# Halves' differences read from PSUM by VectorE, weight low parts issued one by one, and other slots for roundings and maxima

## The chip, the cores and the metric

The kernel runs on one core of one Trainium2 chip. The metric is the device time of one execution in microseconds (us), smaller is better. Engine names are those of the profile: PE is TensorE (PEld its weight loads), DVE is VectorE, ACT is ScalarE, POOL is GpSimd, SP is SyncE, which here issues DMAs alone.

## The reference

A gated linear attention feeds a mixture of experts that is evaluated densely: every token goes through every expert, and a Sinkhorn-balanced matrix `P` weights the outputs.

```python
# attention: batch 4, heads 8, sequence 768, head size 48; f = sigmoid(f_logit)
for t in range(S):
    state = f[:, :, t, :, None] * state + einsum('bhd,bhe->bhde', k[:, :, t], v[:, :, t])
    y[:, :, t] = einsum('bhd,bhde->bhe', q[:, :, t], state)
# experts: x is y as 3072 tokens x 384, 8 experts of 1024 hidden units
logits = x @ w_gate
P = exp(logits - logits.max())
for _ in range(8):
    P /= P.sum(1, keepdims=True) + 1e-9
    P /= P.sum(0, keepdims=True) + 1e-9
    P *= N / E
for e in range(E):
    out += P[:, e:e + 1] * (maximum(x @ w1[e], 0) @ w2[e])
```

## The kernel before

All matrix products run on PE in fp16 with each operand split in a high part (the fp16 rounding, made by ACT) and a low part (what the rounding left, made by DVE or POOL); a product is three matmuls: high x high, high x low, low x high. The names end in h and l for the two parts.

The kernel has three stages. In the first, until about 490 us, the attention runs beside experts 0 and 1, whose outputs go to DRAM and are added later ("readds"). The second and longest is a loop of 48 **periods**, `ORDER`: experts 2 to 7, each in two halves `m` of its hidden units, each half over the four batches `b`. The third is a short tail that finishes the last period's blocks.

A period computes 256 x 768-token work in two layers.

- **Layer one** is a 3x3 block scheme with 15 products in place of 27. `SLOTS` gives their order and the PSUM bank (`kb_A` to `kb_F`) that each is added to: a period has 15 **slots**, one product of 6 matmuls of 256 columns each (two 128-row chunks `c`, three part pairs). Products are used in several sums, so between the slots banks are copied, added and rounded. `EVENTS` says after which slot's matmuls which of these is issued; numbers of 15 and more fall in the next period. Kinds: `copy` (ACT, `cp`), `add`, `init`, `sum` (DVE, from PSUM and a copy), `move` (ACT), `hs` (ACT: relu of a bank to `kr`, fp32), `hh`/`hl` (ACT/DVE: relu's high part `kh` and low part `kl`).
- **Layer two** takes three blocks of tokens `t` (0, 1, 2) per period, each by seven products in place of eight (a 2x2 scheme with halves of 192 columns). It needs sums and differences of halves of the relu: `gs` 1 to 3 (DVE, from the bank and `kr`, to `kr` and `kf`), `gd` (the difference of the two halves of `kr`, on POOL for t = 0 and 1, on DVE for t = 2), `ga`, `gf`, `gb` (`kah` and `kal`, one quarter's parts), and `gh`/`gl` (ACT/POOL: high parts `kgh` and low parts `kgl` of `kr` and `kf`). `paired` is a generator with the products of one block; `advance` steps it twice per slot, the block starting 21, 26 and 31 slots after the period's begin for t = 0, 1, 2. Its results are scaled and added by DVE (`yy`, `acc`), ACT (`xx`, `part`, copies inside `kyps` and `kxps`) and POOL (`acc`).

**Weights** for a later period are prepared meanwhile, on the slots that the plan lists (a list counts from an even period's slot 0 and runs on through the next). `prepare_w1` issues per step: the load (SP); four groups of subtractions (POOL, `k1s`); the maximum (DVE, `wmx`); three steps of high parts (ACT, `k1h`); the low parts `k1l` (DVE): first half of the ten sums, second half, and then both groups of single blocks in one step. `prepare_w2`: load; maximum; two high parts (ACT, `k2h`); two steps of subtractions (POOL, `k2s`); both low parts of single blocks in one step (DVE, `k2l`); high part of the sums; low part of the sums. Periods 0, 1 and 3 have lists of their own, since the loop starts without a store of weights. On the plan stand too the readds (`again`: DMA, ACT `yz`, POOL `acc`), the checks of the inputs' ranges (`checks`) and maxima of the weights of experts 0 and 1 (`maxima`: load in one step, DVE maximum in the next).

What sets the order: every instruction is pinned behind the one issued before it on its engine (`pin`, `mm`), so each engine runs exactly the order in which the code of `period` issues: a slot's matmuls, its events, the first step of the block, the previous period's events that are due (`pending`), the second step of the block, the plan's jobs. Only semaphores hold an engine back. Banks A and F share one PSUM buffer in a period, three such buffers rotate among A, F, E and C; B and D have one each. `kr` has three buffers, `kf` two, raw weights three (`wraw`, shared by loads and `k2s`).

Of the kernel before, what the change touches and what calls it, by code (L numbers as in the profile page):

```python
# [12 lines left out]
ALU = mybir.AluOpType  # L13
# [4 lines left out]
B, H, S, D = 4, 8, 768, 48  # L18
NP = H // 2
C = 64  # L20
# [17 lines left out]
W1S = 2.0 ** 6  # L38
# [26 lines left out]
         (7, 'C', 0), (10, 'D', 0), (8, 'B', 0), (5, 'C', 0), (3, 'D', 0), (14, 'F', 0))  # L65
LAST = (12, 8, 5, 3, 11, 14)
EVENTS = {1: (('copy', 'A', 4),), 2: (('copy', 'B', 13),), 3: (('add', 'A', '-', 13),), 4: (('copy', 'A', 6), ('copy', 'B', 1)),
# [7 lines left out]
END = 24  # L75
ORDER = [(e, m, b) for e in range(2, NE) for m in range(2) for b in range(B)]
PAIRED = (0, 1, 2)
BY_POOL = (1,)
# [180 lines left out]
def fast(ctx, tc, qkf, vbd, wg, w1, w2, out, flag):  # L259
    nc = tc.nc  # L260
# [17 lines left out]
    def pin(ins):  # L278
        engine = ins.ins.engine
        if fixed[0]:  # L280
            if engine in last:
                behind(ins, last[engine])
            last[engine] = ins
        return ins
# [24 lines left out]
    for h in range(2):  # L309
        nc.gpsimd.affine_select(  # L310
            out=mask[h * 64:(h + 1) * 64], in_=mask[h * 64:(h + 1) * 64],
# [701 lines left out]
    def prepare_w1(e, j, cuts=(3, 5, 8)):  # L1013
        raw = raw_weights(e, 1, j)
        yield
        sums = kw.tile([128, 10, 128], F32, name=f"k1s_{e}_{j}", tag="sums", bufs=1)

        def block(v):
            if isinstance(v, str):
                q = int(v[1])  # L1020
                return raw[:, q // 2, 128 * (q % 2):128 * (q % 2) + 128]
            return sums[:, WPOS.index(v), :]

        for part in (WSUMS[i:k] for i, k in zip((0,) + cuts, cuts + (None,))):
            for r, p, op, q in part:
                pin(nc.gpsimd.tensor_tensor(out=block(r), in0=block(p), in1=block(q), op=ALU.add if op == '+' else ALU.subtract))  # L1026
            yield
        pin(nc.vector.tensor_reduce(out=wmx[:, 0, 4 * e + j:4 * e + j + 1], in_=raw.rearrange("p a f -> p (a f)"), axis=AX.X, op=ALU.max, apply_absolute_value=True))
        yield
        wh, wl = (kw.tile([128, PRODUCTS, 128], F16, name=f"k1{n}_{e}_{j}", tag=f"k1{n}") for n in "hl")  # L1030
        halves = ((slice(0, 5), sums[:, 0:5]), (slice(5, 10), sums[:, 5:10]))
        ones = ((slice(10, 12), raw[:, 0:2, 0:128]), (slice(12, 15), raw[:, 0:3, 128:256]))
        for parts in (halves[:1], halves[1:], ones):
            for at_, src in parts:
                pin(nc.scalar.activation(out=wh[:, at_, :], in_=src, func=AF.Copy, scale=W1S))
            yield
        for parts in (halves[:1], halves[1:], ones):
            for at_, src in parts:
                pin(nc.vector.scalar_tensor_tensor(out=wl[:, at_, :], in0=src, scalar=W1S, in1=wh[:, at_, :], op0=ALU.mult, op1=ALU.subtract))  # L1039
            if parts is ones:  # L1040
                k1[e, j] = wh, wl
            yield

    def prepare_w2(e, j):
# [4 lines left out]
        wh, wl = (lp.tile([128, 7, DH], F16, name=f"k2{n}_{e}_{j}", tag=f"k2{n}", bufs=4) for n in "hl")  # L1049
        (b11, b12), (b21, b22) = ((raw[:, f, 0:DH], raw[:, f, DH:DM]) for f in range(2))  # L1050
        pieces = ((wh[:, 0, :], wl[:, 0, :], b11), (wh[:, 1:3, :], wl[:, 1:3, :], raw[:, 1, :].rearrange("p (r d) -> p r d", d=DH)))
# [10 lines left out]
        def lows(parts):  # L1062
            for h_, l_, src in parts:
                pin(nc.vector.scalar_tensor_tensor(out=l_, in0=src, scalar=W2S, in1=h_, op0=ALU.mult, op1=ALU.subtract))  # L1064

        lows(pieces)
        yield
        pin(nc.scalar.activation(out=wh[:, 3:7, :], in_=sums, func=AF.Copy, scale=W2S))
        yield
        lows(((wh[:, 3:7, :], wl[:, 3:7, :], sums),))  # L1070
# [173 lines left out]
    def at_slots(n, slots, gen):  # L1244
        for s in slots:
            plan.setdefault((n, s), []).append(lambda: next(gen, None))

    again = readds()
# [4 lines left out]
    def at_all(n, slots, gen):  # L1253
        for slot in slots:
            at_slots(n + slot // PRODUCTS, (slot % PRODUCTS,), gen)

    for n, (e, m, b) in enumerate(ORDER):
        part = n % 4
        if n + 4 < PERIODS and part in (0, 2):
            e2, m2, _ = ORDER[n + 4]  # L1260
            gen = prepare_w1(e2, 2 * m2 + part // 2)
            at_all(n, (0, 3, 4, 5, 6, 8, 9, 10, 11, 22, 23, 24) if n else (14, 17, 18, 19, 20, 24, 25, 26, 27, 28, 29, 37), gen)
        if n == 0:
            at_all(0, (1, 2, 4, 5, 6, 8, 9, 12), prepare_w2(e, 2 * m))
            at_all(0, (4, 6, 8, 10, 13, 14, 14, 16), prepare_w2(e, 2 * m + 1))
        if n - part + 4 < PERIODS and (n in (1, 3) if n < 4 else part in (0, 2)):
            e2, m2, _ = ORDER[n - part + 4]
            at_all(n, (10, 22, 25, 26, 27, 29, 35, 38) if n != 3 else (0, 2, 8, 12, 13, 16, 17, 20), prepare_w2(e2, 2 * m2 + part // 2))
        if n >= FIRST_READD:
            at_slots(n, (9, 12), again)  # L1270
        if n >= 5 and part in (1, 3):
            for s in (0, 4):
                plan.setdefault((n, s), []).append(lambda: next(checks, None))
        if n >= 6 and part in (0, 2):
            at_slots(n, (1, 9), maxima)
        if n == PERIODS - 2:
            at_slots(n, (1, 2, 3), judged)
    at_all(1, (1, 3, 6, 8, 11, 13, 14, 18, 21, 23, 26, 28, 29), converts[3])
# [11 lines left out]
    def event(ctxt, ev):  # L1290
        banks_, copies, hs, tag = ctxt
# [32 lines left out]
        elif kind == 'gd':  # L1324
            r = hs['r', ev[1]]
            pin((nc.gpsimd if ev[2] == 'P' else nc.vector).tensor_tensor(out=r[:, 0], in0=r[:, 1], in1=r[:, 0], op=ALU.subtract))  # L1326
        elif kind == 'ga':
            hs['a', ev[2]] = [lp.tile([128, 2, 128], F16, name=f"ka{q}_{tag}_{ev[2]}", tag=f"ka{q}{ev[2]}", bufs=1) for q in "hl"]
            pin(nc.scalar.activation(out=hs['a', ev[2]][0], in_=bk[:, :, 0:128], func=AF.Relu))
# [129 lines left out]
```

## Time and profile before

| | |
|---|---|
| median of 3 runs | 1549.83 us (1549.19 to 1549.98) |
| profiled execution, its own time | 1550.04 us |
| its span (first to last instruction) | 1548.3 us |
| granted TensorE clock, mean | 0.996 |
| first write of the period loop to kb_A | 493.39 us |
| start of period 4, of period 46 | 576.40 us, 1475.33 us |

The profile is of one execution. Busy time of an engine leaves out waiting; a matmul's end is modelled, so its row is longer (0.24 to 0.27 us) than the step from one matmul to the next. A timeline row has the start, the duration, engine, line, operation, output and inputs by the program's names, shape, and in brackets the idle time before it with what ended it. A group's row has the count, the busy time, the mean in ns of one, and idle time before it. A wait's row has the total in us, how often, and the longest.

### The profile page before, as it was taken

To read this page: it belongs to the slowest core of one execution; us is meant where nothing else is said; L and a number is where in the kernel's file an instruction comes from. 1 tells how busy PE (TensorE), PEld (TensorE's weight loads), DVE (VectorE), ACT (ScalarE), POOL (GpSimd) and SP (SyncE) were. 2 spreads that over 40 slices of the span, in tenths; PEclk is the share of its full clock that TensorE was granted. 3 is DMA by queue.
4 is the path that set the end of the run, shared out by engine and by line. 5 is a ranking of instruction groups with operands and counts; after the bars stand their busy time and mean duration, and the time that the engine had idled before them with its cause. 6 is when DMAs were issued, how large, how long until landed. Compare 5 with 4: busy or idle time off the path is not lost.

```text
span 1548.3 us, 40171 instructions
## 1 busy us (share of the span) xinstructions
PE 1475.1 (95%) x16051; PEld 1264.8 (82%) x16051; DVE 1315.3 (85%) x2510; ACT 1038.4 (67%) x2310; POOL 1066.0 (69%) x1197
## 2 busy tenths in 40 slices
PE   7899999999999799999999999999999999999996
PEld 4688876676666689898888888898889888988995
DVE  8888888985775998889899999888988989888776
ACT  6655556553344677787777777787777777777772
POOL 1244434546437676989998888898988777887761
PEclk9999999999999999999999999999999999999999
DMA  9455555531000101112221121111111101000011
GB/s 279 118 127 133 126 137 120 142 94 29 31 32 32 32 22 38 44 53 58 62 63 55 40 63 43 48 41 47 47 32 33 32 22 32 22 12 12 2 58 69
DMA packets 82805, 96.00 MB, mean 62 GB/s; under 512 B 49872, under 2 KB 66384, under 8 KB 82608
## 3 DMA queue, kind: packets, MB, share of 16 engines
q1 hardware_dynamic: 82608, 93.34, 21.9%
q8 instruction: 127, 2.08, 0.6%
q14 instruction: 70, 0.57, 0.1%
HBM read 69.53 MB, written 14.16 MB: 54 GB/s over the span
## 4 chain that ended last, share of the span: by engine, by line
PE 54%; DVE 31%; POOL 5%; ACT 5%; issue 4%; DMA 0%; DVEq 0%; POOLq 0%; ACTq 0%
PE kyps L287 13%; PE yps L287 13%; PE hps L287 10%; PE kb_A L287 5%; DVE k1l L1039 4%; PE kb_B L287 4%; DVE kf L1323 3%; DVE kl L1351 2%; POOL kgl L1346 2%; DVE yy L1182 2%; DVE k2l L1064 2%; POOL k1s L1026 2%; DVE kr L1326 2%; PE kb_D L287 2%; DVE kr L1323 2%
## 5 line engine op out<-in xcount | busy, mean ns | idle before, releaser
L287 PEld LDWEIGHTS <-k1h 128*128 128x128 f16 x2880 | 282.0, 98 | 40.5 <-DVE kl L1351 11.2
L287 PE MATMUL kyps<-k2h,kgh 128*128 128x192 f16 x1152 | 283.6, 246 | 1.0 <-ACT kyps L1179 1.0
L287 PE MATMUL kyps<-k2l,kgh 128*128 128x192 f16 x1152 | 283.7, 246 | 0.0
L287 PE MATMUL kyps<-k2h,kgl 128*128 128x192 f16 x1152 | 283.7, 246 | 0.0
L287 PEld LDWEIGHTS <-kgh 128*128 128x128 f16 x2304 | 216.8, 98 | 3.2
L1346 POOL TENSOR_TENSOR kgl<-kr,kgh 128x512 f16<-128x512 f32 x141 | 166.5, 1181 | 48.5 <-ACT kgh L1343 48.4
L1346 POOL TENSOR_TENSOR kgl<-kf,kgh 128x512 f16<-128x512 f32 x141 | 180.3, 1279 | 4.7 <-ACT kgh L1343 4.7
L1182 DVE SCALAR_TENSOR_TENSOR yy<-kyps,pes,part 128x192 f32<-128x192 f32 x264 | 108.3, 410 | 85.3 <-PE kyps L287 82.7
L287 PEld LDWEIGHTS <-k1l 128*128 128x128 f16 x1440 | 141.0, 98 | 38.3 <-issue 28.5
L1218 POOL TENSOR_TENSOR acc<-acc,yy 128x384 f32<-128x384 f32 x129 | 141.4, 1096 | 42.0 <-DVE yy L1182 42.0
L287 PE MATMUL yps<-w2h,hl 128*128 128x384 f16 x384 | 125.2, 326 | 4.0 <-DVE hl L440 3.8
L287 PE MATMUL yps<-w2l,hh 128*128 128x384 f16 x384 | 125.1, 326 | 2.3 <-DVE w2l L359 2.3
L287 PEld LDWEIGHTS <-w1h 128*128 128x128 f16 x1344 | 97.3, 98 | 34.9 <-issue 4.0
L287 PE MATMUL yps<-w2h,hh 128*128 128x384 f16 x384 | 125.1, 326 | 0.2 <-ACT hh L437 0.2
L1179 ACT ACTIVATE kxps<-kyps 128x192 f32<-128x192 f32 x144 | 46.6, 324 | 105.4 <-DVE acc L1182 58.7
L287 PEld LDWEIGHTS <-kgl 128*128 128x128 f16 x1152 | 112.8, 98 | 4.6 <-issue 1.2
L287 PEld LDWEIGHTS <-hh 128*128 128x128 f16 x768 | 74.5, 98 | 48.1 <-issue 2.9
L287 PEld LDWEIGHTS <-kh 128*128 128x128 f16 x1152 | 108.3, 98 | 3.2
L1218 POOL TENSOR_TENSOR acc<-acc,xx 128x384 f32<-128x384 f32 x43 | 43.0, 1000 | 74.8 <-ACT xx L1179 74.8
L287 PE MATMUL kyps<-k2h,kh 128*128 128x192 f16 x288 | 70.7, 246 | 22.5 <-DVE yy L1182 21.0
L1343 ACT ACTIVATE kgh<-kr 128x512 f16<-128x512 f32 x144 | 90.7, 630 | 2.0 <-DVE kr L1323 1.9
L1343 ACT ACTIVATE kgh<-kf 128x512 f16<-128x512 f32 x144 | 90.5, 629 | 0.3 <-PE kyps L287 0.3
(298 smaller groups left out, 5406.9 us busy)
## 6 DMA issues: line engine op xcount, KB each, us to landing
q<-in_qkf_dram SPq DMA_DIRECT2D x23, 672.0 KB, 5.1
vr<-in_vbd_dram SPq DMA_DIRECT2D x24, 384.0 KB, 3.7
k1r<-in_w_dram SPq DMA_DIRECT2D x24, 384.0 KB, 3.0
ys<-yr SPq DMA_DIRECT2D x48, 192.0 KB, 2.8
k2r<-in_w_dram SPq DMA_DIRECT2D x24, 384.0 KB, 3.1
yb<-ys SPq DMA_DIRECT2D x48, 192.0 KB, 2.4
out_dram<-acc SPq DMA_DIRECT2D x24, 192.0 KB, 1.9
w1r<-in_w_dram SPq DMA_DIRECT2D x8, 384.0 KB, 10.7
```

The source lines that it names most:

```text
L287: ins = (nc.tensor.transpose if transpose else nc.tensor.matmul)(**kw)
L1026: pin(nc.gpsimd.tensor_tensor(out=block(r), in0=block(p), in1=block(q), op=ALU.add if op == '+' else ALU.subtract))
L1039: pin(nc.vector.scalar_tensor_tensor(out=wl[:, at_, :], in0=src, scalar=W1S, in1=wh[:, at_, :], op0=ALU.mult, op1=ALU.subtract))
L1064: pin(nc.vector.scalar_tensor_tensor(out=l_, in0=src, scalar=W2S, in1=h_, op0=ALU.mult, op1=ALU.subtract))
L1179: pin(nc.scalar.activation(out=out, in_=in_, func=AF.Copy, **kw))
L1182: pin(nc.vector.scalar_tensor_tensor(out=y, in0=ps, scalar=p, in1=z, op0=ALU.mult, op1=ALU.add))
L1218: pin((nc.vector if n == len(ORDER) - 1 else nc.gpsimd).tensor_tensor(out=y, in0=y, in1=z.rearrange("p s d -> p (s d)"), op=ALU.add))
L1323: pin(nc.vector.scalar_tensor_tensor(out=out, in0=bk[:, :, 128 * v:128 * v + 128], scalar=0.0, in1=other, op0=ALU.max, op1=op))
L1326: pin((nc.gpsimd if ev[2] == 'P' else nc.vector).tensor_tensor(out=r[:, 0], in0=r[:, 1], in1=r[:, 0], op=ALU.subtract))
L1343: pin(nc.scalar.activation(out=hs['g', t][0][i], in_=hs['f' if i else 'r', t], func=AF.Copy))
L1346: pin((nc.vector if tag == str(PERIODS - 1) else nc.gpsimd).tensor_tensor(out=hs['g', t][1][i], in0=hs['f' if i else 'r', t], in1=hs['g', ...
L1351: pin(nc.vector.scalar_tensor_tensor(out=hl, in0=bk, scalar=0.0, in1=hh, op0=ALU.max, op1=ALU.subtract))
```

## The change

- A new event kind `gp` replaces `gd` for t = 0 and t = 2: DVE computes the difference from the bank's second half and the first half of `kr` in one pass. `gd` stays for t = 1, on POOL.
- `EVENTS`: init E one slot later; ga A and hs A together at slot 8; copy of C and gf A at slot 9; hh B and init F at slot 11; hs E at slot 12; the three `gs` of B over slots 12 and 13; `gd` 1 at 14; `gl` 0 0 from slot 14 to 16; `gh` 2 0 from 22 to 21; `gl` 1 0 from 19 to 21, `gl` 1 1 from 20 to 22, `gl` 2 0 from 22 to 26; `hl` C between two `gs` at slot 18.
- `prepare_w1` issues its four low parts in four steps, `prepare_w2` its two low parts of single blocks in two.
- The plan's slots become named lists with other values; readds move from slots 9 and 12 to 9 and 14, checks from 0 and 4 to 3 and 3, maxima from 1 and 9 to 0 and 5.

```diff
-          5: (('init', 'E', '-', 6, 'D'),), 6: (('copy', 'A', 0),), 7: (('add', 'B', '+', 0),), 8: (('move', 'C', 'B'), ('hs', 'A', 0)),
-          9: (('ga', 'A', 0), ('gd', 0, 'P')), 10: (('copy', 'C', 7), ('gf', 'A', 0)), 11: (('add', 'D', '-', 7), ('hs', 'E', 1)),
-          12: (('init', 'F', '+', 1, 'D'), ('hh', 'B', 0), ('ga', 'E', 1)), 13: (('gs', 'B', 0, 1), ('gs', 'B', 0, 2), ('gs', 'B', 0, 3), ('gb', 1, 'P'), ('gd', 1, 'P')),
-          14: (('gh', 0, 0), ('gl', 0, 0), ('sum', 'D', '-', 4, 3), ('hl', 'B', 0)), 15: (('add', 'C', '+', 3), ('hh', 'D', 2), ('gh', 0, 1), ('gl', 0, 1)),
-          16: (('hs', 'F', 2), ('hh', 'C', 1), ('hl', 'D', 2)), 17: (('ga', 'F', 2), ('gd', 2, 'V'), ('gs', 'D', 2, 1), ('gs', 'D', 2, 2), ('gs', 'D', 2, 3)),
-          18: (('gs', 'C', 1, 1), ('gs', 'C', 1, 2), ('gs', 'C', 1, 3), ('hl', 'C', 1), ('gf', 'F', 2)), 19: (('gh', 1, 0), ('gl', 1, 0)),
-          20: (('gh', 1, 1), ('gl', 1, 1)), 22: (('gh', 2, 0), ('gl', 2, 0)), 23: (('gh', 2, 1), ('gl', 2, 1))}
-END = 24
+          6: (('copy', 'A', 0), ('init', 'E', '-', 6, 'D')), 7: (('add', 'B', '+', 0),), 8: (('move', 'C', 'B'), ('ga', 'A', 0), ('hs', 'A', 0)),
+          9: (('copy', 'C', 7), ('gp', 'A', 0), ('gf', 'A', 0)), 11: (('add', 'D', '-', 7), ('hh', 'B', 0), ('init', 'F', '+', 1, 'D')),
+          12: (('hs', 'E', 1), ('ga', 'E', 1), ('gs', 'B', 0, 1)), 13: (('gs', 'B', 0, 2), ('gs', 'B', 0, 3), ('gb', 1, 'P')),
+          14: (('gh', 0, 0), ('sum', 'D', '-', 4, 3), ('hl', 'B', 0), ('gd', 1, 'P')),
+          15: (('add', 'C', '+', 3), ('hh', 'D', 2), ('gh', 0, 1), ('gl', 0, 1)),
+          16: (('hs', 'F', 2), ('hh', 'C', 1), ('gl', 0, 0), ('hl', 'D', 2), ('gp', 'F', 2)),
+          17: (('ga', 'F', 2), ('gs', 'D', 2, 1), ('gs', 'D', 2, 2), ('gs', 'D', 2, 3)),
+          18: (('gs', 'C', 1, 1), ('gs', 'C', 1, 2), ('hl', 'C', 1), ('gs', 'C', 1, 3), ('gf', 'F', 2)), 19: (('gh', 1, 0),), 20: (('gh', 1, 1),),
+          21: (('gh', 2, 0), ('gl', 1, 0)), 22: (('gl', 1, 1),), 23: (('gh', 2, 1), ('gl', 2, 1)), 26: (('gl', 2, 0),)}
+END = 27
+W1AT = (1, 3, 4, 5, 5, 5, 10, 10, 11, 21, 23, 24, 25)
+W1AT0 = (16, 17, 17, 19, 20, 22, 22, 23, 25, 26, 26, 33, 37)
+W2AT = (8, 22, 23, 24, 27, 29, 30, 37, 38)
+W2AT0 = (0, 1, 5, 6, 7, 8, 9, 11, 13)
+W2AT1 = (7, 8, 8, 12, 12, 12, 14, 14, 18)
+W2AT3 = (2, 3, 11, 16, 17, 19, 19, 20, 24)
+READDAT = (9, 14)
+CHECKAT = (3, 3)
+MAXAT = (0, 5)
 ...
-        for parts in (halves[:1], halves[1:], ones):
-            for at_, src in parts:
-                pin(nc.vector.scalar_tensor_tensor(out=wl[:, at_, :], in0=src, scalar=W1S, in1=wh[:, at_, :], op0=ALU.mult, op1=ALU.subtract))
-            if parts is ones:
+        for at_, src in halves + ones:
+            pin(nc.vector.scalar_tensor_tensor(out=wl[:, at_, :], in0=src, scalar=W1S, in1=wh[:, at_, :], op0=ALU.mult, op1=ALU.subtract))
+            if src is ones[1][1]:
                 k1[e, j] = wh, wl
             yield
 ...
-        lows(pieces)
-        yield
+        for piece in pieces:
+            lows((piece,))
+            yield
 ...
-            at_all(n, (0, 3, 4, 5, 6, 8, 9, 10, 11, 22, 23, 24) if n else (14, 17, 18, 19, 20, 24, 25, 26, 27, 28, 29, 37), gen)
+            at_all(n, W1AT if n else W1AT0, gen)
-            at_all(0, (1, 2, 4, 5, 6, 8, 9, 12), prepare_w2(e, 2 * m))
-            at_all(0, (4, 6, 8, 10, 13, 14, 14, 16), prepare_w2(e, 2 * m + 1))
+            at_all(0, W2AT0, prepare_w2(e, 2 * m))
+            at_all(0, W2AT1, prepare_w2(e, 2 * m + 1))
-            at_all(n, (10, 22, 25, 26, 27, 29, 35, 38) if n != 3 else (0, 2, 8, 12, 13, 16, 17, 20), prepare_w2(e2, 2 * m2 + part // 2))
+            at_all(n, W2AT if n != 3 else W2AT3, prepare_w2(e2, 2 * m2 + part // 2))
-            at_slots(n, (9, 12), again)
+            at_slots(n, READDAT, again)
-            for s in (0, 4):
+            for s in CHECKAT:
-            at_slots(n, (1, 9), maxima)
+            at_slots(n, MAXAT, maxima)
 ...
+        elif kind == 'gp':
+            r = hs['r', ev[2]]
+            pin(nc.vector.scalar_tensor_tensor(out=r[:, 0], in0=bk[:, :, 128:256], scalar=0.0, in1=r[:, 0], op0=ALU.max, op1=ALU.subtract))
```

## The prediction

> **What bounds the kernel now.** I read the page's first part, then a table of stretches, then who waited for whom in the steady stage, then single instructions. Page, busy time by engine:
>
> ```profile
> span 1548.3 us, 40171 instructions
> PE 1475.1 (95%) x16051; PEld 1264.8 (82%) x16051; DVE 1315.3 (85%) x2510; ACT 1038.4 (67%) x2310; POOL 1066.0 (69%) x1197
> ```
>
> TensorE carries the span. The change touches only the stage of 48 periods, which begins at 493.39 us; I cut it at first writes to kb_A (columns: stretch, length, then busy time of PE, PEld, DVE, ACT, POOL):
>
> ```profile
> 493.39:576.40 83.01, 71.17 (x680) 63.13 (x679) 71.62 (x132) 57.72 (x127) 50.86 (x62) 0.96 0.09 27
> 576.40:1475.33 898.93, 869.27 (x9074) 805.05 (x9073) 796.88 (x1572) 682.57 (x1571) 760.89 (x867) 1.00 0.13 39
> 1049.91:1070.62 20.71, 20.54 (x219) 19.22 (x217) 17.98 (x37) 17.85 (x40) 19.39 (x26) 1.00 0.17 50
> 1070.62:1092.80 22.18, 20.95 (x219) 19.12 (x218) 20.23 (x40) 15.65 (x38) 19.37 (x20) 1.00 0.15 45
> 1475.33:1495.55 20.22, 20.22 (x219) 19.19 (x217) 15.13 (x41) 14.08 (x33) 12.74 (x14) 1.00 0.17 60
> 1515.77:1541.43 25.66, 17.27 (x194) 15.79 (x191) 20.60 (x53) 8.93 (x23) 4.15 (x5) 1.00 0.20 72
> ```
>
> These are periods 0 to 3; periods 4 to 45; the even period 26; the odd period 27; period 46, in which no weights are prepared; and the tail after the last kb_F product. Period 46 shows the floor: 20.22 us with PE never idle, at a granted clock of 1.00. The 42 periods of the second row take 898.93 - 42 x 20.22 = 49.7 us more than that, 2.37 per pair. An even period loses 0.49, an odd one 1.96. Periods 0 to 3 hold 83.01 - 71.17 = 11.8 us of PE idle, the tail 8.4. Nothing beyond these 70 us can be won, and no single engine but PE is full: DVE is at 89% in the steady stage. So what matters is which DVE pass comes late. Waits of PE, then of its weight loads, in the steady stage:
>
> ```profile
> PE kyps L287 <- DVE yy L1182: 15.8, 21, 1.3
> PE kb_A L287 <- ACT cp L1300: 5.0, 21, 0.3
> PE kb_D L287 <- DVE kb_F L1305: 3.8, 20, 0.2
> ```
> ```profile
> PEld L287 <- DVE kl L1351: 6.6, 19, 0.4
> ```
>
> The idle times start at modelled matmul ends, so by starts they are some 0.16 us longer each. The first row is the odd period's: DVE brings the yy of slot 10 too late for the products of slot 12. The timeline of DVE in odd period 25, and PE beside it:
>
> ```profile
> 1039.87 0.42 DVE L1182 SCALAR_TENSOR_TENSOR yy<-kyps,pes,part 128x192 f32<-128x192 f32 x1 [1.42 <-PE kyps L287]
> 1040.20 0.41 DVE L1182 SCALAR_TENSOR_TENSOR acc<-kyps,pes,acc 128x192 f32<-128x192 f32 x1
> 1040.53 0.81 DVE L1039 SCALAR_TENSOR_TENSOR k1l<-k1s,k1h 128x640 f16<-128x640 f32 x1
> 1041.26 0.95 DVE L1047 TENSOR_REDUCE wmx<-k2r 128x1 f32<-128x768 f32 x1
> 1042.12 0.81 DVE L1039 SCALAR_TENSOR_TENSOR k1l<-k1s,k1h 128x640 f16<-128x640 f32 x1
> 1042.85 2.38 DVE L1039 SCALAR_TENSOR_TENSOR k1l<-k1r,k1h 128x256 f16<-128x256 f32 x2
> 1045.16 0.41 DVE L1332 SCALAR_TENSOR_TENSOR kal<-kb_A,kah 128x256 f16<-128x256 f32 x1
> 1045.49 0.40 DVE L1182 SCALAR_TENSOR_TENSOR acc<-kxps,pes,acc 128x192 f32<-128x192 f32 x1
> 1045.82 0.40 DVE L1182 SCALAR_TENSOR_TENSOR yy<-kyps,pes,part 128x192 f32<-128x192 f32 x1
> 1046.14 0.68 DVE L1302 TENSOR_TENSOR kb_D<-kb_D,cp 128x512 f32<-128x512 f32 x1
> 1046.86 0.70 DVE L1305 TENSOR_TENSOR kb_F<-kb_D,cp 128x512 f32<-128x512 f32 x1
> ```
> ```profile
> 1045.31 0.27 PE L287 MATMUL kb_C<-xal,k1h 128*128 128x256 f16 x1
> 1046.27 0.24 PE L287 MATMUL kyps<-k2h,kh 128*128 128x192 f16 x1 [0.69 <-DVE yy L1182]
> 1047.61 0.27 PE L287 MATMUL kb_D<-xah,k1h 128*128 128x256 f16 x1 [0.19 <-DVE kb_F L1305]
> ```
>
> DVE idles 1.42 us, then runs 7.7 us without a gap, with all four k1l low parts in the middle; PE stops twice behind it, at slot 12 (yy) and at slot 13 (kb_F).
>
> **The change part by part.** *The differences.* Per period, 'gd' 0 leaves POOL and 'gd' 2 leaves DVE; each becomes a 'gp' on DVE that reads the bank. The rows for both forms, in the steady stage; gp is nearest to the kr<-kb_D pass, of the same shapes:
>
> ```profile
> L1326 DVE TENSOR_TENSOR kr<-kr 128x256 f32<-128x256 f32 x42 | 36.0, 858 | 6.7 <-ACT kr L1315 6.7
> L1323 DVE SCALAR_TENSOR_TENSOR kr<-kb_D,kr 128x256 f32<-128x256 f32 x42 | 17.8, 425 | 1.4
> L1039 DVE SCALAR_TENSOR_TENSOR k1l<-k1r,k1h 128x256 f16<-128x256 f32 x20 | 27.2, 1358 | 0.0
> L1039 DVE SCALAR_TENSOR_TENSOR k1l<-k1r,k1h 128x384 f16<-128x384 f32 x20 | 21.8, 1090 | 0.0
> ```
> ```profile
> L1326 POOL TENSOR_TENSOR kr<-kr 128x256 f32<-128x256 f32 x83 | 66.7, 804 | 3.2
> ```
>
> DVE: -0.858 + 2 x 0.425, so nothing in total; POOL: -0.80 per period. But the place matters. The old pass varies widely; in odd period 27 it was long, and stands right before the chain to kb_A of slot 5:
>
> ```profile
> 1073.86 1.40 DVE L1326 TENSOR_TENSOR kr<-kr 128x256 f32<-128x256 f32 x1 [0.35 <-ACT kr L1315]
> ```
>
> There 1.40 becomes 0.42. The gp of F keeps the wait of that row: it stands at slot 16, ACT's kr of F ends it, and the gs of D, yy and kb_A's add are queued behind it on DVE, as they were behind gd; the gp of A at slot 9 waits for ACT's kr of A, which ends a slot before. Nothing is added for either, at most the 0.35 of the row per period.
>
> The Trainium skill, page "SBUF — State Buffer", section "Who interferes with whom", says that a VectorE instruction with two SBUF inputs and a GpSimd instruction that reads SBUF block each other whole, while one with a single SBUF input goes free. The spread of kr<-kr against the steady 0.42 of the PSUM form agrees; by that rule alone gp would keep 0.42 under any POOL load, the value that the row gives as well.
>
> *k1l apart (slots 22, 23, 24 to 21, 23, 24, 25).* In the odd period the first half goes to slot 6, into the 1.42 us idle (start to start 1041.26 - 1040.53 = 0.73, cover 1.42); the last part goes behind the yy of slot 10 (about 1.0 by its row); gp of A enters at slot 9 (start to start 0.33, as kal's). yy ends 0.73 + 1.0 - 0.33 = 1.40 earlier: 1046.22 becomes 1044.82, before PE is free at 1045.31 + 0.11 = 1045.42. The wait of 0.85 at slot 12 goes. Next late is kb_F: everything still lies ahead of it, so it gains 0.73 - 0.33 = 0.40 only, to 1047.16. PE would be there at 1045.42 + 0.99 = 1046.41 (period 46, 20.22 us, is 90 matmuls of 0.11 and 126 of 0.082, so 12 products take 0.99). So slot 13 waits 0.75 where the two places together cost 1047.61 - 1046.41 = 1.20. Moving init F to slot 11 changes nothing here, as DVE had nothing between it and the add.
>
> *Odd period, the rest: 1.96 - 1.20 = 0.76* (kb_A at slot 5, kb_B at slot 1 behind kl). kb_A's chain loses 1.0 of gd; kl of B no longer stands behind POOL's kr, and one 'gs' moves from slot 13 to 12. I take both as gone.
>
> *Even period: 0.49.* The second k2l piece moves behind the add to C, so the copies of slots 2 to 4 are earlier; but it stays ahead of kb_A's add. I keep 0.35 at slot 5, and 0.1 for init E, now at slot 6 behind two maxima moved to slot 5 where DVE was idle.
>
> The k1l and k2l parts alone may each meet a POOL instruction, where two of them now stand back to back (1.36 and 1.09 above show that they already do). I put 0.1 more on the odd chain. A pair then loses 0.75 + 0.1 + 0.35 + 0.1 = 1.3 in place of 2.37: 1.07 x 21 = 22 us. Ends: nothing gained (0) and all of it (49.7).
>
> *POOL's lows.* 'gl' 1 0, 1 1, 2 0 go two to four slots later, ten k1s subtractions come first; costed at nothing, the cover is in the second rival. ACT's reordering ('ga', 'hh B', copy of C one slot earlier) fills idle time of an engine at 76% of the stage; nothing. DMA: loads of W1 at slot 1, maxima at slot 0, W2 at slot 8; SP only waits for a free buffer, and k1r's is freed by the k2l piece at slot 0, one slot before. k1s lies two slots behind it on POOL. Nothing, up to 1 us per even period if POOL waits.
>
> *Periods 0 to 3.* New slots spread W2's passes (old: a maximum at slot 2 of period 3, ahead of kb_A's add). Of 11.8 idle I take 3, between -3 and 8.
>
> *Tail.* Low parts of t=1 stood before the yy that PE waits for:
>
> ```profile
> 1526.11 0.24 PE L287 MATMUL kyps<-k2h,kh 128*128 128x192 f16 x1 [1.97 <-DVE yy L1182]
> ```
>
> They go one slot behind it; 1.97 at most, some returns; I take 1.5, from -1 to 4.
>
> Sum: 22 + 3 + 1.5 = 26.5. The profiled execution took 1550.04 us (1.7 around its span), 0.2 above the median of 1549.83, so 1523.5 in either.
>
> **The rivals.** *1. The low parts, standing alone, meet POOL each time.* For: kr<-kr at 858 on average; against: half parts at 0.81 with POOL busy. Three parts on the odd chain (second half, both others) each longer by 0.25 make 0.75, of which 0.1 is in the sum: 0.65 x 21 = 14 back, 1537. The skill's lock rule would do just this, as a pass with two SBUF inputs that starts behind POOL waits for the whole instruction.
>
> *2. Slower: kgl of t=1 too late in even periods.* Rows of POOL in period 26:
>
> ```profile
> 1059.55 1.15 POOL L1346 TENSOR_TENSOR kgl<-kr,kgh 128x512 f16<-128x512 f32 x1
> 1060.66 0.44 POOL L1026 TENSOR_TENSOR k1s<-k1s,k1r 128x128 f32<-128x128 f32 x1
> ...
> 1062.71 1.17 POOL L1026 TENSOR_TENSOR k1s<-k1s 128x128 f32<-128x128 f32 x1
> ```
> PE's slot 11 there began with this row:
> ```profile
> 1065.03 0.27 PE L287 MATMUL kb_B<-xah,k1h 128*128 128x256 f16 x1
> 1065.14 0.27 PE L287 MATMUL kb_B<-xah,k1l 128*128 128x256 f16 x1
> ```
>
> It ended at 1060.70 after three k1s. With all ten first it ends seven later: six near 0.44 and one of 1.17, some 3.8, at 1064.5. PE needs it in the second product of slot 11: 1065.03 + 6 x 0.11 + 6 x 0.082 = 1066.2, about 0.6 earlier with what PE gains until there (0.45 of odd period 25, 0.14 of 26). The margin is 1.1 us. POOL 2.9 us later (two kgl and a k1s more ahead of it) would cost 1.8 x 21 = 38 us: 1562. Against: POOL loses a kr pass (0.80) per period, and nothing new stands ahead of that kgl but the k1s.
>
> *3. The wait only moves.* If slot 13 takes all that slot 12 gave, and slot 5 stays: 1549. For: DVE runs 7.7 us without a gap; against: 0.73 of it goes into idle time.
>
> **How the numbers follow.** The sum 0.74, the first rival 0.12, no change 0.06, the slower one 0.08. A gain of 14 us less reaches 1538, of 4 us in all 1546; the other end, a pair that keeps 0.6, gains 37 + 5 and gives 1508. The range 1507 to 1544 leaves about 2 in 10 out. Differences under 0.2% (3 us) can't be told here. Faster 0.86 (the first two), same 0.06, slower 0.08.
>
> **What would show it.** Right: kyps <- yy nearly gone in the steady stage, kb_D <- kb_F larger (some 0.6 by its row per odd period); no DVE kr<-kr; the reading of the bank near 425 ns; POOL's kr<-kr 48, not 96; odd periods near 21.1 us, even near 20.7. Wrong: a row PE kyps <- POOL kgl; k1l parts of 640 elements well over 0.83 us; kb_E or kb_C waited for in even periods; periods 0 to 3 above 83 us.

## The result and the profile after

The kernel after takes 1492.34 us (median of 4 runs, 1491.92 to 1492.5) against 1549.51 (1548.87 to 1549.98): a ratio of 0.963, 95% interval 0.961 to 0.965. It is faster, as forecast, but by 57 us where 26.5 were forecast, and below the range of 1507 to 1544.

The first part of its page:

```profile
span 1490.5 us, 40081 instructions
PE 1453.7 (98%) x16051; PEld 1265.0 (85%) x16051; DVE 1283.4 (86%) x2558; ACT 1035.7 (69%) x2310; POOL 1010.9 (68%) x1149
```

PE does the same matmuls and is busy 98% of a shorter span. The stretches that answer to those of before (periods 0 to 3; 4 to 45; odd period 25; even period 26; 46; from period 47's start to the last product; columns as before):

```profile
496.25:570.72 74.47, 67.46 (x679) 61.31 (x678) 67.40 (x136) 57.75 (x127) 43.06 (x54) 1.00 0.10 31
570.72:1421.73 851.01, 850.08 (x9076) 806.53 (x9073) 770.53 (x1615) 679.54 (x1571) 717.45 (x828) 1.00 0.14 41
997.11:1017.33 20.22, 20.22 (x218) 19.20 (x217) 18.91 (x40) 15.64 (x38) 16.57 (x18) 1.00 0.14 41
1017.33:1037.55 20.22, 20.22 (x218) 19.19 (x217) 17.91 (x40) 17.56 (x41) 19.80 (x25) 1.00 0.20 60
1421.73:1441.95 20.22, 20.22 (x219) 19.20 (x217) 15.21 (x43) 14.35 (x33) 12.09 (x13) 1.00 0.17 61
1441.95:1483.75 41.80, 37.49 (x409) 34.98 (x407) 32.63 (x83) 23.27 (x56) 15.81 (x17) 1.00 0.20 73
```

Odd and even periods now take the floor of 20.22 us. The 57.8 us of span divide into: steady stage 898.93 to 851.01, -47.9 (42 periods at the floor of 20.22 are 849.2, so 1.8 are left above it); periods 0 to 3 -8.5; from period 47's start to the last product 44.63 to 41.80, -2.8; behind the last product -1.4 (not taken apart); and ahead of the loop, which begins at 496.25 in place of 493.39, +2.9. The next two rows are all that PE still waits for an engine in the steady stage, where before had rows of 15.8, 5.0 and 3.8 us and one of 6.6 for the weight loads:

```profile
PE kyps L298 <- DVE yy L1193: 0.6, 1, 0.6
PE kb_C L298 <- ACT kb_C L1319: 0.3, 1, 0.3
```

Where the odd period's 2 us went is seen on DVE and POOL side by side. First POOL beside the DVE rows of period 25 that the prediction shows, and the 128x256 low part of that stretch alone; then DVE and POOL in the same period after:

```profile
1042.16 1.79 POOL L1346 TENSOR_TENSOR kgl<-kf,kgh 128x512 f16<-128x512 f32 x1
1042.85 1.38 DVE L1039 SCALAR_TENSOR_TENSOR k1l<-k1r,k1h 128x256 f16<-128x256 f32 x1
1043.92 0.90 POOL L1326 TENSOR_TENSOR kr<-kr 128x256 f32<-128x256 f32 x1
```
```profile
1008.49 0.42 DVE L1193 SCALAR_TENSOR_TENSOR yy<-kyps,pes,part 128x192 f32<-128x192 f32 x1
...
1010.01 0.81 DVE L1049 SCALAR_TENSOR_TENSOR k1l<-k1s,k1h 128x640 f16<-128x640 f32 x1
1010.74 0.41 DVE L1340 SCALAR_TENSOR_TENSOR kr<-kb_A,kr 128x256 f32<-128x256 f32 x1
1011.08 0.41 DVE L1346 SCALAR_TENSOR_TENSOR kal<-kb_A,kah 128x256 f16<-128x256 f32 x1
1011.41 0.72 DVE L1049 SCALAR_TENSOR_TENSOR k1l<-k1r,k1h 128x256 f16<-128x256 f32 x1
1012.05 0.41 DVE L1193 SCALAR_TENSOR_TENSOR acc<-kxps,pes,acc 128x192 f32<-128x192 f32 x1
1012.38 0.40 DVE L1193 SCALAR_TENSOR_TENSOR yy<-kyps,pes,part 128x192 f32<-128x192 f32 x1
1012.70 0.84 DVE L1049 SCALAR_TENSOR_TENSOR k1l<-k1r,k1h 128x384 f16<-128x384 f32 x1
1013.46 0.69 DVE L1313 TENSOR_TENSOR kb_D<-kb_D,cp 128x512 f32<-128x512 f32 x1
1014.18 0.70 DVE L1316 TENSOR_TENSOR kb_F<-kb_D,cp 128x512 f32<-128x512 f32 x1
```
```profile
1010.42 1.43 POOL L1360 TENSOR_TENSOR kgl<-kf,kgh 128x512 f16<-128x512 f32 x1 [0.43 <-ACT kgh L1357]
1011.81 1.32 POOL L1067 TENSOR_TENSOR k2s<-k2r 128x192 f32<-128x192 f32 x2
```

Read the ends. Before, POOL's kgl ends at 1042.16 + 1.79 = 1043.95 and the 128x256 pass, begun 1.10 earlier, at 1044.23, 0.28 behind it. POOL's kr follows to 1044.82, and the 128x384 pass ends at 1042.85 + 2.38 = 1045.23, 0.41 behind that. The two engines took turns: one's instruction stands until the other's has ended, which is called a lock below. After, kgl ends at 1011.85 and the 128x256 pass at 1012.13: 0.28 again. The k2s pair ends at 1013.13 and the 128x384 pass at 1013.54: 0.41 again. What differs is how much of POOL's instruction is left when the pass begins, because after the sums' low part DVE first does two passes that read a bank (kr and kal), which run at 0.41 us while POOL works. POOL's kgl itself ended 1.02 us behind the sums' low part before (1043.95 - 1042.93) and 1.03 after, so POOL takes the same time in both. From yy's start to kb_F's end it was 7.69 us before, and is 1014.88 - 1008.49 = 6.39 after.

This holds all through: in the 12 runs in which these passes have two SBUF inputs, 239 of the 240 passes of 128x256 in the steady stage began while POOL worked, and each ended 278 to 288 ns behind POOL's instruction, however long that lasted. All 960 `k1l` passes of these stages can be priced so: a pass takes its own length (0.41 us for 128x256, 0.54 for 128x384, 0.81 for 128x640) or what is left of POOL's instruction plus 0.28, 0.42 or 0.68 us, whichever is longer. This fits 941 of them within 20 ns. The other 19 (16 in one run, 3 in another) began at most 31 ns after POOL's instruction; they kept their own length, and POOL's instruction was the one that grew (128x192 k2s 1.02 us, and 0.59 where the order was the other way).

### The profile page after: what moved, and what is told of

Its sections match the earlier page's. It is cut to its first block, busy times and chain, and to the rows that moved or that the text cites. A ratio compares the mean times of both kernels' runs of the same rounds, so it can differ in the third digit from the quotient of the medians.

```text
span 1490.5 us, 40081 instructions
## 1 busy us (share of the span) xinstructions
PE 1453.7 (98%) x16051; PEld 1265.0 (85%) x16051; DVE 1283.4 (86%) x2558; ACT 1035.7 (69%) x2310; POOL 1010.9 (68%) x1149
## 4 chain that ended last, share of the span: by engine, by line
PE 62%; DVE 2%; ACT 0%; issue 0%; DVEq 0%; ACTq 0%
PE kyps L298 28%; PE kb_B L298 8%; PE kb_A L298 8%; PE kb_D L298 6%; PE kxps L298 5%; PE kb_C L298 4%; PE kb_E L298 2%; PE kb_F L298 2%; DVE yy L1193 0%; DVE kf L1334 0%; DVE kl L1365 0%; DVE acc L1193 0%; DVE k1l L1049 0%; DVE kgl L1360 0%; DVE kr L1334 0%
## 5 line engine op out<-in xcount | busy, mean ns | idle before, releaser
L1360 POOL TENSOR_TENSOR kgl<-kf,kgh 128x512 f16<-128x512 f32 x141 | 172.5, 1224 | 31.0 <-ACT kgh L1357 24.1
L1360 POOL TENSOR_TENSOR kgl<-kr,kgh 128x512 f16<-128x512 f32 x141 | 180.7, 1282 | 12.7 <-ACT kgh L1357 12.7
L1229 POOL TENSOR_TENSOR acc<-acc,yy 128x384 f32<-128x384 f32 x129 | 129.1, 1001 | 72.7 <-DVE yy L1193 72.5
L1190 ACT ACTIVATE kyps<-kyps 128x192 f32<-128x192 f32 x144 | 46.6, 324 | 76.0 <-PE kyps L298 76.0
L1311 ACT ACTIVATE cp<-kb_A 128x512 f32<-128x512 f32 x144 | 86.2, 599 | 2.3 <-PE kb_A L298 1.2
L298 PE MATMUL hps<-xh,w1h 128*128 128x128 f16 (+1 forms) x672 | 83.9, 257 | 3.0 <-DVE hl L402 2.6
```

The lines of the kernel that those rows point to most:

```text
L298: ins = (nc.tensor.transpose if transpose else nc.tensor.matmul)(**kw)
L1190: pin(nc.scalar.activation(out=out, in_=in_, func=AF.Copy, **kw))
L1229: pin((nc.vector if n == len(ORDER) - 1 else nc.gpsimd).tensor_tensor(out=y, in0=y, in1=z.rearrange("p s d -> p (s d)"), op=ALU.add))
L1311: pin(nc.scalar.activation(out=fresh(ev[2]), in_=bk, func=AF.Copy))
L1360: pin((nc.vector if tag == str(PERIODS - 1) else nc.gpsimd).tensor_tensor(out=hs['g', t][1][i], in0=hs['f' if i else 'r', t], in1=hs['g', ...
```

## The experiments

**Undo the separation.** The kernel after, with the parts still separate instructions but issued in one slot, so that they stand back to back (W1's second half moves with them, from slot 23 to 24):

```diff
-W1AT = (1, 3, 4, 5, 5, 5, 10, 10, 11, 21, 23, 24, 25)
-W2AT = (8, 22, 23, 24, 27, 29, 30, 37, 38)
+W1AT = (1, 3, 4, 5, 5, 5, 10, 10, 11, 21, 24, 24, 24)
+W2AT = (8, 22, 23, 24, 27, 29, 29, 37, 38)
```

> The changed kernel with the parts issued back to back again: second half and both single groups of k1l in one place (slot 24), both single pieces of k2l in one place (slot 29); everything else as changed. Theory A (a k1l or k2l pass straight behind another one lets POOL in between and waits for POOL's whole instruction): k1l 256 and 384 grow from 719 and 839 ns to about 1360 and 1090, k2l 192 and 384 from 357 and 847 to about 760 and 1030, PE waits at slots 12 and 13 of odd periods again, 15 to 25 us over the changed kernel: about 1512. Theory B (POOL has less to do since the difference left it, so the passes are short wherever they stand): lengths stay within 10%, the chain to slot 13 is no longer than now, 1492 to 1495. Theory C (the slots, not the lengths): lengths stay, and yy of slot 10 is 0.84 us later, which its slack of about 1.2 us covers: 1493 to 1498.

1511.4 us, ratio 0.975 (0.974 to 0.977). This is theory A's time, 19 us of the gain, but not its passes: the 128x256 group is at 808 ns, and the first of the three W1 parts pays.

```profile
L1049 DVE SCALAR_TENSOR_TENSOR k1l<-k1s,k1h 128x640 f16<-128x640 f32 x40 | 60.0, 1500 | 0.0
```
```profile
1020.38 1.16 POOL L1360 TENSOR_TENSOR kgl<-kf,kgh 128x512 f16<-128x512 f32 x1 [0.42 <-ACT kgh L1357]
```
```profile
1020.64 1.59 DVE L1049 SCALAR_TENSOR_TENSOR k1l<-k1s,k1h 128x640 f16<-128x640 f32 x1
1022.15 0.81 DVE L1049 SCALAR_TENSOR_TENSOR k1l<-k1r,k1h 128x256 f16<-128x256 f32 x1
```

The second half now begins 0.26 us after kgl's start and ends 1022.23 - 1021.54 = 0.69 after its end. So "a low part behind another" is not the rule: whichever begins while POOL works, waits. Theory A's condition falls, theories B and C fall with the time, and what stays is A's lock.

**The separation alone.** The kernel before, with the low parts one by one (W1's at 22, 23, 24, 25, W2's at 29, 30).

> The kernel before with one thing of the change: the low parts one by one (W1 at 22, 23, 24, 25, W2 at 29, 30; in periods 0 to 3 at the old places; the preparation ahead of the loop as before). Theory A: k1l 256 still follows the second half directly and stays near 1360 ns, k1l 384 now follows yy and falls to about 840, k2l 192 stays where it follows kl and k2l 384 falls to about 850; the wait at slot 12 goes, that at slot 13 stays near 0.9 us: 10 to 18 us faster, about 1535. Theory B: no length changes by more than 10%, the wait only moves from slot 12 to slot 13: 1543 to 1549. Theory C: as B.

1547.7 us, ratio 0.998 (0.9975 to 0.9994): nearly nothing, within theory B's range, although the 128x384 part falls to 883 ns as theory A said. The wait moves, as the prediction's third rival said for the whole change:

```profile
PE kb_D L287 <- DVE kb_F L1306: 17.4, 20, 1.2
```

The 128x256 part still follows the second half directly and stays at 1359 ns.

**The differences back.** The kernel after, with `gd` 0 on POOL and `gd` 2 on DVE:

```diff
-('gp', 'A', 0)
+('gd', 0, 'P')
-('gp', 'F', 2)
+('gd', 2, 'V')
```

> The changed kernel with both differences as before (t=0 on POOL at slot 9, t=2 on VectorE from kr alone at slot 16). Theory A: the k1l and k2l passes stay short (720 to 850 ns); the pass kr<-kr stands behind a pass from PSUM and takes 0.5 to 0.9 us; the wait at slot 5 returns in part: 0 to 8 us over the changed kernel. Theory B: POOL's 0.8 us per period come back, k1l and k2l go back to 1000 to 1360 ns and the waits with them: 1515 to 1540.

1504.9 us, ratio 0.971 (0.969 to 0.973): they are worth 12.6 us here, between the two theories' ranges; the 128x256 part is 1049 ns long and the 128x384 one 630. DVE waits for POOL's difference before it can do the `gs` behind it, and PE and its weight loads for the kl of B behind that (3.6 and 7.0 us):

```profile
DVE kr L1334 <- POOL kr L1337: 35.8, 19, 2.1
```

**The differences alone, two ways.** The kernel before with `gp` in the places of `gd`, behind ACT's `ga`; and with `gp` ahead of `ga`:

```diff
-          9: (('ga', 'A', 0), ('gd', 0, 'P')),
+          9: (('ga', 'A', 0), ('gp', 'A', 0)),        # second run: (('gp', 'A', 0), ('ga', 'A', 0))
-          17: (('ga', 'F', 2), ('gd', 2, 'V'), ...
+          17: (('ga', 'F', 2), ('gp', 'F', 2), ...    # second run: gp F as the last of slot 16
```

> The kernel before with one thing of the change: both differences read from PSUM on VectorE (t=0 at slot 9, t=2 at slot 17). Theory A: k1l and k2l keep 1360, 1090, 760 and 1030 ns; only the waits at slots 5 and 1 go, the odd chain grows by 0.33: 5 to 12 us faster, about 1541. Theory B: k1l and k2l fall by a third or more, 15 to 30 us faster, about 1527.

1581.8 us, ratio 1.021 (1.019 to 1.023): 32 us slower, which no theory had. The longest wait of DVE and that of PE in its steady stage:

```profile
DVE kr L1329 <- ACT kah L1332: 67.2, 45, 2.2
```
```profile
PE kb_D L287 <- DVE kf L1323: 21.4, 42, 0.6
```

DVE's reading of bank F waits for ACT's reading of the same bank, which was issued before it and stands late in ACT's queue: all 42 readings of F in the stage waited, 65.7 us in all, and one of A.

> The kernel before with both differences read from the bank, as in the run that gave 1581.8 us, but the reading of A issued ahead of ga A at slot 9 and that of F at slot 16, ahead of ga F at 17. In that run DVE waited 43 times, 64.0 us in all, in kr<-kb_F for ACT's kah<-kb_F, which reads the same bank and was issued before it. Theory (order of two readers of a bank): this wait is the whole loss of 32 us; with the reading ahead it goes, kb_D <- DVE kf at slot 4 (0.71 us per even period, 0.65 per odd one) goes, and the time is 1540 to 1552 us. Rival (the pass itself is dear in this place, whoever reads the bank): kb_D <- DVE kf stays and the time stays over 1570.

1528.9 us, ratio 0.987 (0.985 to 0.988): 53 us from two places in the order, better than expected. The low parts fell too, the 128x256 one from 1358 to 1014 ns and the 128x384 one from 1090 to 705: POOL's kr of t = 0 is gone, and 12 of 20 passes of 128x384 begin with POOL idle. The wait is now ACT's, which has the time:

```profile
ACT kah L1332 <- DVE kr L1329: 66.9, 41, 2.0
```

So here two readings of one bank by two engines run in the order of issue; the pass itself is cheap (415 ns). The Trainium skill, "PSUM — Partial Sum Buffer", section "PSUM bank collisions raise a hardware error", says that the compiler's scheduler makes two instructions of different engines on one bank and one group of 32 partitions depend on each other, reads as well; these two runs agree (67.2 us of DVE behind ACT, then 66.9 of ACT behind DVE). Alone and well placed, the differences give 21 us.

**Events and lists apart.** The kernel after with the events of before (but `gp` at 9 and 16 ahead of `ga`), and with the lists of before (W1's parts at 22 to 25, W2's at 29 and 30, loads, readds, checks, maxima on their old slots):

> The kernel after with the order of events of before; only the two readings of the bank stay (A at slot 9, F at slot 16, each ahead of ACT's second reading of the bank). The plan's lists are those of after. Theory (the lists carry the gain, the events little): at most 0.3 us per period comes back, at slot 5 of even and slot 1 of odd periods, 1492 to 1505 us. Rival (the later kgl roundings of t=1 and 2 and the spread kr and kf passes carry it): 1515 us and more, with kb_A <- ACT cp or kb_D <- DVE kb_F waited for in nearly every period.

1509.3 us, ratio 0.974 (0.972 to 0.975). Even periods take 20.74, odd ones 20.22 but for a few; the wait of 0.39 at slot 5 of even periods is back:

```profile
PE kb_A L296 <- ACT cp L1309: 4.6, 20, 0.2
```

There the 128x384 part of W2 takes 1.27 us beside a kgl begun 0.30 before it, `gl` 0 0, which the change has moved two slots on; after, it takes 0.85 beside a kr of 0.73:

```profile
1028.60 1.16 POOL L1358 TENSOR_TENSOR kgl<-kr,kgh 128x512 f16<-128x512 f32 x1
```
```profile
1028.90 1.27 DVE L1072 SCALAR_TENSOR_TENSOR k2l<-k2r,k2h 128x384 f16<-128x384 f32 x1
```

It also begins 0.53 us later in its period (2.32 against 1.79 us), so that `gl` 0 0 alone makes the wait is argued, not shown. The theory was 4 us short, and the rival's price too high.

> The kernel after with the plan's lists of before in the steady stage (low parts of W1 at 22, 23, 24 and 25, of W2's single blocks at 29 and 30, loads, maxima, readds, checks on their old slots); the events are those of after. Theory (lock, and the lists decide how much of a POOL instruction is left when a low part begins): the second half of the sums and the 128x256 part follow each other directly at slots 8 and 9 of the odd period, one of them is 0.5 us longer or more, kyps <- DVE yy or kb_D <- DVE kb_F comes back at slots 12 and 13 with 0.3 us or more per odd period, 1503 to 1525 us. Rival (the differences and the events carry the gain): 1492 to 1496 us.

1520.6 us, ratio 0.981 (0.979 to 0.983): even periods are at 20.22, odd ones at 21.6, and the wait is at slot 13, 1.1 us per odd period:

```profile
PE kb_D L298 <- DVE kb_F L1316: 18.7, 20, 1.0
```

The time is in the theory's range, but another pass pays. The 128x256 part, now behind kr and kal, is short (617 ns); the first half, back on its old slot, stands in the odd chain again, beside POOL:

```profile
1022.04 1.00 POOL L1229 TENSOR_TENSOR acc<-acc,yy 128x384 f32<-128x384 f32 x1 [1.85 <-DVE yy L1193]
```
```profile
1022.20 1.52 DVE L1049 SCALAR_TENSOR_TENSOR k1l<-k1s,k1h 128x640 f16<-128x640 f32 x1
```

From yy's start (1021.54) to kb_F's end (1029.34) the chain is 7.80 us long, against 6.39 in the kernel after.

Taken out of the whole, the lists cost 28 us, the events 17, the differences 12.6, the separation 19; put into the kernel before alone, the differences give 21 and the separation 2. They overlap and depend on each other: they don't add up to 57. By kind of period they part more clearly. Even periods take 20.74 us with the old events and are on average within 0.1 of the floor with the old lists, the parts back to back or the old differences. Odd ones rise to 21.6 with the old lists, 21.1 with the parts back to back and 20.8 with the old differences, and most stay at 20.22 with the old events.

**Is it a lock?** The kernel before with the k1l passes from one SBUF input (the subtraction of the high part is left out); in the second of two runs the 128x256 one takes three blocks of 128 in place of two:

```diff
-pin(nc.vector.scalar_tensor_tensor(out=wl[:, at_, :], in0=src, scalar=W1S, in1=wh[:, at_, :], op0=ALU.mult, op1=ALU.subtract))
+pin(nc.vector.tensor_scalar(out=wl[:, at_, :], in0=src, scalar1=W1S, scalar2=None, op0=ALU.mult))
+                if at_.start == 10:      # second run, ahead of it
+                    at_, src = slice(10, 13), raw[:, 0:3, 0:128]
```

> The kernel before, with the k1l passes computed from the weights alone (a scaling, one SBUF input; the subtraction of the high part is left out, so W1's low parts are not the reference's). Theory (lock): a pass with two SBUF inputs that starts while a POOL instruction runs ends a fixed time after that instruction (in the traces so far 0.28 us for 128x256, 0.42 for 128x384, 0.68 for 128x640, all 20 passes of a kind within 7 ns), so its length is mostly POOL's rest. With one input the passes fall to about 0.3, 0.45 and 0.7 us whatever POOL does, the odd period's chain of 7.69 us to kb_F loses 1.7, the waits at slots 12 and 13 go (1.2 to 1.5 us per odd period), and the time is 1515 to 1527 us. Rival (POOL and DVE share a bandwidth, so any pass beside POOL is slow): the 128x256 and 128x384 passes stay at 1.0 us or more, the odd period above 21.8, the time above 1543.

1530.4 us, ratio 0.987 (0.986 to 0.989), 3 us above the range expected. One pass did not fall:

```profile
L1039 DVE TENSOR_SCALAR k1l<-k1r 128x256 f16<-128x256 f32 x20 | 24.6, 1228 | 0.0
L1039 DVE TENSOR_SCALAR k1l<-k1s 128x640 f16<-128x640 f32 x40 | 20.1, 503 | 0.0
L1039 DVE TENSOR_SCALAR k1l<-k1r 128x384 f16<-128x384 f32 x20 | 10.8, 539 | 0.0
```

The 128x384 pass fell from 1090 to 539 ns with POOL busy past its end. The 128x256 one still ends behind POOL. 128x640 in 503 ns is faster than 128x384, so it runs in another mode. The Trainium skill, "VectorE: DVE Perf Modes", section "Mode 2×_2P", says that a one-source pass between SBUF operands reads through both ports, two elements per cycle, when the outermost dimensions of source and destination are both even or equal, and "SBUF — State Buffer", section "Who interferes with whom", that this mode contends with GpSimd for ports that the two engines share. The destination is one run of 256 or 384 elements; of the sources, two blocks are even, three are neither even nor equal to 384 (the five of 128x640 adjoin, one run of 640).

The one pass isn't what missed the range, as the run after this one shows, where it is short and the time the same. The odd periods did what the theory said: they fall from 22.03 to 20.87 us on average, and the rows of slots 12 and 13 are gone but for one wait. The even ones grew from 20.77 to 21.11, 7 us in all, with a wait of PE that the kernel before doesn't have and whose cause is open:

```profile
PE kb_B L287 <- ACT cp L1300: 4.0, 20, 0.2
```

> The kernel before with the k1l passes from one input, as in the run that gave 1530.4 us (the subtraction of the high part is left out), and the 128x256 one widened to three blocks of 128 columns in place of two (the third is overwritten by the next pass). In that run the 128x256 pass of two blocks still ended a fixed 0.15 us after POOL's instruction (1.23 us long), while the 128x384 pass of three blocks took 0.54 us in all 20 periods although POOL ran on past its end. Theory (two even blocks let the pass run at two elements per cycle through a second port, which POOL has to give up first; three blocks do not): the widened pass takes 0.54 us beside the same POOL instruction. Rival (the place decides: the pass that begins right behind POOL's start waits, whatever its form): it stays at 1.2 us or more. The time says little, 1525 to 1532 us, since PE waited elsewhere in that run.

1530.4 us, ratio 0.987 (0.986 to 0.989), and the pass in three blocks, beside the same kgl:

```profile
1030.82 1.46 POOL L1348 TENSOR_TENSOR kgl<-kf,kgh 128x512 f16<-128x512 f32 x1
```
```profile
1031.18 0.54 DVE L1041 TENSOR_SCALAR k1l<-k1r 128x384 f16<-128x384 f32 x1
```

It ended 0.56 us before POOL did, with half as many elements again as the pass that waited. So the form of the pass decides, and not the place or a shared bandwidth. That what the two engines share is a port is the two pages' account; both runs agree with it.

**Ahead of the loop.** The kernel after with the last two k1l parts in one step for the preparations ahead of the loop; the kernel after unchanged beside it; and the first with period 0's lists for W2 as before:

> The kernel after, with the last two k1l parts in one step for the two preparations ahead of the loop alone, as before; in the loop they stay apart. Theory: the extra steps there cost the 2.86 us by which the loop of the kernel after begins later (496.25 against 493.39 us); the loop begins at 493.4 again and the time is 1489.5 us. Rival: the start of the loop stands behind another engine, the loop begins at 496 and the time is 1492.3; or periods 0 to 3 (74.47 us) give back what the start gains, with the same time.

> The kernel after, unchanged, beside the run before it on the same chip: 1492.3 us, 0.963 of before. What differs from it in the run before is the step ahead of the loop alone.

1491.8 us (ratio 0.9624, 0.9611 to 0.9637) beside 1492.8 (0.9632, 0.9619 to 0.9645). The loop begins at 495.19 against 495.97 (496.25 in the first profile): the step was 0.8 of the 2.9 us, not all.

> The kernel after with the last two k1l parts joined ahead of the loop, and with period 0's two lists for W2 as before (1, 2, 4, 5, 6, 8, 8, 9, 12 and 4, 6, 8, 10, 13, 14, 14, 14, 16). With the joined step alone the loop began at 495.19 us, against 495.97 of the kernel after beside it and 493.39 of before; what still differs there is four k2s passes on POOL, which stand among the last k1s at 458 to 463 us, where before has them at 473 to 478. Theory: these passes are the rest of the late start; the loop begins at 493.2 to 493.8, and if periods 0 to 3 keep their 75 us the time is 1489 to 1491. Rival: W2's early passes are what made periods 0 to 3 shorter (83.0 before, 74.5 after): they grow by more than the 1.8 us won, and the time is 1492 to 1498.

1491.5 us, ratio 0.9622 (0.9609 to 0.9635). The loop begins at 492.95, so period 0's lists for W2 were the rest. Its four k2s passes stand at 473 to 478 us again, as in the kernel before; that they are what delayed the loop was not tried alone. Its first stretches:

```profile
492.95:569.35 76.40, 69.77 (x679) 62.29 (x678) 68.10 (x136) 57.81 (x127) 42.83 (x54) 0.96 0.10 30
569.35:1420.35 851.00, 850.07 (x9075) 806.53 (x9073) 770.68 (x1615) 678.79 (x1571) 717.39 (x828) 1.00 0.15 41
```

Periods 0 to 3 give back 1.9 of the 3.0 us, all of it in period 1: 23.13 us at a granted clock of 0.85, against 21.24 at 1.00 in the unchanged kernel beside the run before. How much of it is the clock's is open. By its interval this version can't be told from the kernel after.

## Why the forecast was right in direction and wrong in size

- *The step that failed is "k1l apart".* It costed the last part at "about 1.0 by its row" and left the 128x256 part at 1.36, as if a pass had a length of its own beside POOL. What the runs showed in its place is the longer of the pass's own length and what is left of POOL's instruction plus a fixed part. Start to start, the two passes went from 1.31 and 1.00 us to 0.64 and 0.76: 0.9 us less on the odd chain, forecast 7.69 - 0.40 = 7.29, measured 6.39. With it "slot 13 waits 0.75" plus "0.1 more on the odd chain" came out as nothing: 0.85 x 21 = 17.9 us of the miss. What the step said of the wait at slot 12 was right: it is gone.
- *"I keep 0.35 at slot 5, and 0.1 for init E"* in even periods: also nothing, 9.5 us. The run with the old events has that wait back and those with the old lists or with the parts back to back have not, so the events carried it. The event that its trace points to, `gl` 0 0 two slots later, is not in the prediction: its part on POOL's lows, "costed at nothing", takes three others. The two terms are 1.3 x 21 = 27.3; less the 1.8 still above the floor they make 25.5, and the steady stage was missed by 47.9 - 1.07 x 21 = 25.4.
- *The first rival* had the lock and the wrong sign: parts standing alone do meet POOL, but they wait for what is left of its instruction, and behind a pass from PSUM less is left than behind another low part. The sign of being wrong that the prediction named for the 128x640 parts did come, 1102 ns in place of 833:

```profile
L1049 DVE SCALAR_TENSOR_TENSOR k1l<-k1s,k1h 128x640 f16<-128x640 f32 x40 | 44.1, 1102 | 0.0
```

The second halves are at 0.81; 18 of the 20 first halves meet a kgl at their new slot and take 1.10 to 1.61 us. PE doesn't wait behind them, as that slot lies ahead of the chain, where DVE had idled.
- *The Trainium skill's lock rule* ("SBUF — State Buffer", section "Who interferes with whom") stood in the prediction for kr<-kr and for that rival, not for the rows 1358 and 1090 themselves, which it explains. It says that a VectorE pass with two SBUF inputs and a GpSimd instruction that reads SBUF contend, under an exclusive lock, and that a pass with one SBUF input does not unless it runs in a two-port mode. The passes measured here agree: of the first kind one engine waited for the other, and gp, with one input in PSUM, kept its 415 ns.
- *The differences*: gp at 415 ns as forecast, POOL's kr<-kr at 41 in the stage in place of 83. That gp of F must stand ahead of ACT's second reading of the bank was not seen. The change has it so (for A it puts ga ahead of hs, on which gp waits in any case); the other order cost 53 us in the kernel before.
- *Periods 0 to 3*: 3 forecast, 8.5 measured, half a microsecond outside the end given. Periods 1 and 2 of before had granted clocks of 0.92 and 0.93, which the profiled run after does not have:

```profile
505.62:528.17 22.55, 17.75 (x158) 14.81 (x156) 21.48 (x38) 18.73 (x39) 17.85 (x22) 0.92 0.18 53
528.17:552.76 24.59, 22.05 (x218) 20.34 (x217) 21.14 (x42) 16.24 (x38) 16.80 (x24) 0.93 0.01 2
```

That is 0.08 x 22.55 + 0.07 x 24.59 = 3.5 us at most, an estimate, and so much of the 8.5 may be no gain of the change; the rest was not taken apart.

- *Tail*: 1.5 forecast, 2.8 measured; the wait of 1.97 fell to 0.25 (third row after), the first one with it by 1.26, and ACT's copy took 0.47 more. The first waits of PE in the tail, before (two, ahead of the one in the prediction) and after:

```profile
1519.32 0.24 PE L287 MATMUL kyps<-k2h,kh 128*128 128x192 f16 x1 [1.90 <-DVE yy L1182]
1522.49 0.24 PE L287 MATMUL kyps<-k2h,kgh 128*128 128x192 f16 x1 [1.04 <-ACT kyps L1179]
```

```profile
1464.45 0.24 PE L298 MATMUL kyps<-k2h,kh 128*128 128x192 f16 x1 [0.64 <-DVE yy L1193]
1468.10 0.24 PE L298 MATMUL kyps<-k2h,kgh 128*128 128x192 f16 x1 [1.51 <-ACT kyps L1190]
1470.00 0.24 PE L298 MATMUL kyps<-k2h,kh 128*128 128x192 f16 x1 [0.25 <-DVE yy L1193]
```

- *Ahead of the loop*: 2.9 us lost, not in the prediction; the preparation's steps run there too, and "The change touches only the stage of 48 periods" was wrong.
- *The slower rival* (kgl of t=1 late) did not come: there is no row of PE waiting for kgl. *The third* is what the separation alone does.

Odd periods were forecast near 21.1 us and even ones near 20.7, and both are 20.22. The range went to 1507 because it kept 0.6 us per pair of periods; 0.1 is left. The end "all of it", which the prediction named at 49.7 us, was the case.

## What to carry to other kernels

A VectorE pass with two SBUF inputs that begins while GpSimd works cost, in all these runs, the rest of GpSimd's instruction plus a fixed part, and its own length only where that was longer or where the two began at the same moment and it went first. So price it from the two engines' rows side by side, never from its mean. Put a pass that reads PSUM between two such passes, so that GpSimd's instruction runs out under it, and look again at every other slot when one is moved. Where two engines read one bank, issue first the one whose queue is urgent.

## What the runs showed of the hardware

- A pass with two SBUF inputs begun under a POOL instruction, with more than 0.15 us of that left, ended behind it by 0.28 us (128x256), 0.42 (128x384) and 0.68 (128x640), within 11 ns of each other for a size, over 12 runs. The exceptions are 19 passes begun at most 31 ns after POOL's instruction, for which POOL's gave way. POOL's kgl likewise ended 1.03 behind the DVE pass that it met (1011.85 - 1010.82).
- One input does not free a pass by itself: 1228 ns in two blocks, 544 in three, in the same place.
- The order of two readings of a bank moved the kernel from 1581.8 to 1528.9 us.
